# A fused attention and two-layer kernel: three-part storage of the combined weights, a step plan for the output weights and first operands, and the second group's weights fetched first

## The chip, the cores and the metric

One Trainium2 chip, one core. The metric is the device time of one execution in microseconds (us), as the median of several runs. One further execution was taken with the hardware profiler; its rows are the evidence here. Engines: PE is TensorE, ACT is ScalarE, DVE is VectorE, POOL is GpSimd, SP is SyncE, which only issues DMAs here, in the order of the program.

## The reference, cut to what matters

```python
# q, k, v, alpha: (4, 8, 768, 48)
for t in range(S):
    state = alpha[:, :, t, :, None] * state + einsum('bhd,bhe->bhde', k[:, :, t], v[:, :, t])
    y[:, :, t] = einsum('bhd,bhde->bhe', q[:, :, t], state)
x = y.transpose(0, 2, 1, 3).reshape(3072, 384)
h = x @ w_in                                   # w_in (384, 2048)
x = (h * sigmoid(h)) @ w_out                   # w_out (2048, 384)
g = x @ w_gate                                 # w_gate, w_val (384, 1536)
return (g * sigmoid(g) * (x @ w_val)) @ w_out2 # w_out2 (1536, 384)
```

## The kernel before, in words

The 24 chunks of 128 tokens form seven blocks (j = 0 to 6, of 4, 3, 3, 3, 3, 4, 4 chunks). The first layer walks blocks and 16 slices f of w_in and w_out: `g1` makes h of a slice in nine matmuls, `act1` makes silu(h) twice on ACT (`gh`, rounded, and `h`) and DVE forms the remainder `gl`; `g2` multiplies w_out with `gh` (six matmuls) and `gl` (three). PE runs g1 one step ahead of g2: g1(s+1), g2(s), g1(s+2), g2(s+1). A step has two half steps, `slot(s, 0)` before g2 and `slot(s, 1)` after it; hs = 2f + half numbers them in a block. Work for other stages is written into these slots by hand. All engines run their instructions in program order, so an instruction that waits holds up what stands behind it on its engine. Every operand is kept as two float32r parts, high and low; ACT writes a high part, DVE or POOL the low part by subtraction.

The second layer's gate and value products are done as a bilinear scheme: for each of eight groups (NG2 = 8) nine 128x128 weight tiles become 15 combined tiles (5 of part A, 10 of part B), with 15 products per token pair instead of 18. Three pieces of work prepare it, and the change touches all of them.

- **Combined weights** (`combs`, called in each half step of blocks 2 to 5, here a tick; 15 ticks make one group u, k is the tick in it). `load2` brings a raw 64-bit weight unit on SP into one of two raw buffers, `decode2` turns it into float32 on DVE in three instructions (steps 0, 1, 2), `combine` adds tiles on POOL, `high_comb` copies 5 or 10 tiles to a result tile on ACT, `low_comb` makes the remainder on POOL, and `keep_comb` stores the tile to HBM (`comb_d`). All these result tiles of a block share one SBUF buffer, so `high_comb` of one part waits until the store of the part before it has landed. Part A is copied at k = 9 and stored at k = 12; part B is copied at k = 0 of the next group and stored at k = 4.
- **Output weights** (`units_o`, last block, j = 6): 12 units. In one half step DVE decodes a unit, in the next ACT makes the high and POOL the low part; SP stores it in the step after and loads another raw unit behind the store.
- **First operands** (`moving`, last block): 15 operands of 512 tokens for the first token pair from six slices of x: 10 sums (a1 to a10), 15 high copies (h0 to h14) and 15 low parts (l0 to l14). They are taken from the list `MOVING`, two per half step from hs = 5 to 24: sums on POOL, high on ACT, low parts with an odd number on DVE and with an even one on POOL.

`flag` in the last block (hs = 14) sums a range check on PE into PSUM bank 5, DVE copies it to `bad`, and three one-off matmuls (`bits`) then write banks 5, 6 and 7.

The second layer follows an ordered list of events (`GATE`, `VALUE`, due times in the list's own unit). `run(until)` emits the events that are due; near the end of block 6 it is called several times, so that products of group 0 (`p5`, `p0`, `p7` ...; three matmuls each) fall between the last g1 and g2. When block 6 is done, `wstack.close()` frees the first layer's weights, and `fetch(1)`, `fetch(2)`, `fetch(3)` bring the combined weights of groups 1 to 3 into three `ring` buffers that lie in that place. Group 0's were fetched in pieces before (`fetch_first`). The last block's own result goes to HBM (`x1_d`) from `g2` before these fetches are issued.

Of the kernel before, what the change touches and what calls it, by code (L numbers as in the profile page):

```python
# [10 lines left out]
F32 = mybir.dt.float32  # L11
# [9 lines left out]
DM = H * D  # L21
# [247 lines left out]
def fast(ctx, tc, pk, w1, w2, out, bad_i):  # L269
# [464 lines left out]

    def g2(j, f):
# [114 lines left out]
    comb_a, comb_b = {}, {}  # L850

    def high_comb(u, j, keep, n, src):
        t = big((0, 2, 1)[j % 3], f"comb{u}_{n}", F32R)[:, :2 * n * 128]
        t = keep[u] = t.rearrange("p (x i e) -> p x i e", x=2, i=n)
        ACT.activation(out=t[:, 0], in_=src, func=AF.Copy)

    def low_comb(t, src, lo, hi):
        sub(POOL, t[:, 1, lo:hi], src[:, lo:hi], t[:, 0, lo:hi])

    def keep_comb(u, t, lo, hi):  # L860
        SP.dma_start(
            out=comb_d[u, :, 128 * lo:128 * hi], in_=t.bitcast(F32).rearrange("p x i e -> p (x i e)")
        )

    comb_tick = [0]

    def combs(j):

        t, comb_tick[0] = comb_tick[0], comb_tick[0] + 1
        u, k = divmod(t, 15)  # L870
        if t == 0:
            load2(0)
            load2(1)
        if 0 < u <= NG2:
            if k == 0:
                high_comb(u - 1, j, comb_b, 10, fcomb)
            if 1 <= k <= 3:
                low_comb(comb_b[u - 1], fcomb, *((0, 3), (3, 6), (6, 10))[k - 1])
            if k == 4:
                keep_comb(u - 1, comb_b.pop(u - 1), 10, 30)  # L880
        if u >= NG2:
            return
        if k < 9:
            decode2(3 * u + k // 3, k % 3)
# [4 lines left out]
        if k == 9:  # L889
            high_comb(u, j, comb_a, 5, fa[:, :5])  # L890
        for name in {6: ("b1", "b2"), 7: ("b3", "b4"), 8: ("b5",), 9: ("c1", "c2"), 11: ("c3",),
                     12: ("c4", "c5"), 13: ("c6", "c7"), 14: ("c8", "c9")}.get(k, ()):
            combine(name)
        if k == 10:
            low_comb(comb_a[u], fa, 0, 3)
        if k == 11:
            low_comb(comb_a[u], fa, 3, 5)
        if k == 12:
            keep_comb(u, comb_a.pop(u), 0, 10)


    wo_tick, wo_raw, wo_t = [0], [], {}

    def units_o():

        t, wo_tick[0] = wo_tick[0], wo_tick[0] + 1
        f, k = divmod(t, 2)
        key = "2", NW + f
        if t == 0:
            area = big(1, "wo", F32R).rearrange("p (i c) -> p i c", i=4)  # L910
            wo_raw.extend(raw2 + [area[:, i].bitcast(I32) for i in (2, 3)])
            wo_t.update({i: area[:, i] for i in range(2)})
            for i in range(4):
                load_unit(("2", NW + i), w2_src(NW + i), wo_raw[i])
        if k == 0 and 0 < f <= NF2:
            SP.dma_start(out=wo_d[f - 1], in_=wo_t[(f - 1) % 2].bitcast(F32))
            if f + 3 < NF2:
                load_unit(("2", NW + f + 3), w2_src(NW + f + 3), wo_raw[(f + 3) % 4])
        if f >= NF2:
            return  # L920
        if k == 0:
            for i in range(3):
                decode_unit(key, i)
        else:
            to = wo_t[f % 2]
            ACT.activation(out=to[:, :DM], in_=raw_t[key], func=AF.Copy)
            sub(POOL, to[:, DM:], raw_t.pop(key), to[:, :DM])

# [6 lines left out]
    def fetch(n):  # L935
# [4 lines left out]
        if i < NG2:  # L940
            SP.dma_start(out=t.bitcast(F32), in_=comb_d[i])
            a = t[:, :10 * 128].rearrange("p (x i e) -> p x i e", x=2, i=5)
            b = t[:, 10 * 128:].rearrange("p (x i e) -> p x i e", x=2, i=10)
            comb_t[p, i] = lambda x, r: a[:, x, PART_A[r]] if r in PART_A else b[:, x, PART_B[r]]
# [15 lines left out]

    first_comb = {}

    def fetch_first(k):
        src = comb_d[0]
        if k == 0:
            t = first_comb[0] = cw.tile([128, 10, 128], F32R, tag="fcomb", name="first0")
            SP.dma_start(
                out=t.bitcast(F32).rearrange("p i e -> p (i e)"), in_=src[:, :10 * 128]
            )
        elif k == 1:  # L970
            t = first_comb[1] = mp.tile([128, 2, 4, 128], F32R, tag="y3", name="first1", bufs=1)
            for x in range(2):
                lo = (10 + 10 * x) * 128
                SP.dma_start(
                    out=t[:, x].bitcast(F32).rearrange("p i e -> p (i e)"), in_=src[:, lo:lo + 4 * 128]
                )
        else:
            for x in range(2):
                t = first_comb[2 + x] = cw.tile(
                    [128, 6, 128], F32R, tag=f"raw2_{x}", name=f"first{2 + x}"  # L980
                )
                lo = (14 + 10 * x) * 128
                SP.dma_start(
                    out=t.bitcast(F32).rearrange("p i e -> p (i e)"), in_=src[:, lo:lo + 6 * 128]
                )

    def first_view(x, r):
        if r in PART_A:
            return first_comb[0][:, 5 * x + PART_A[r]]
        i = PART_B[r]  # L990
        return first_comb[1][:, x, i] if i < 4 else first_comb[2 + x][:, i - 4]
# [158 lines left out]
    events.sort(key=lambda e: e[0])  # L1150

# [172 lines left out]
    def start_phase2():  # L1324
# [3 lines left out]
        assert comb_tick[0] > 15 * NG2 + 3  # L1328
# [19 lines left out]
    def flag():  # L1348
# [5 lines left out]
        for i in (5, 6, 7):  # L1354
            PE.matmul(
                bank(i, f"bits{i}"), part(unit_t["1", 2 * NF1 - 1], 0), x_t[NB1 - 1][:, 0, 0],
                start=True, stop=True,
            )

    def slot(s, half, first=None):  # L1360
# [24 lines left out]
        if j == NB1 - 1:  # L1385
            units_o()
# [6 lines left out]
            if hs == 26:  # L1393
# [8 lines left out]
    todo = [op for op, _ in MOVING]  # L1402
# [7 lines left out]
    for s, (j, f) in enumerate(steps):  # L1410
# [20 lines left out]
    for n in range(1, 4):  # L1431
        fetch(n)
# [86 lines left out]
```

## Time and profile before

| what | value |
|---|---|
| time before, median of 3 runs | 994.44 us (991.08 to 996.62) |
| the profiled execution, time | 992.06 us |
| its span (first to last instruction) | 990.3 us |
| mean granted TensorE clock | 0.980 |
| busy PE / DVE / ACT / POOL | 930.5 / 623.0 / 449.1 / 319.3 us |

The profiled execution lies 2.4 us below the median of the runs. Times in rows count from the start of the span. PE is busy 94% of the span, so what can be won lies in its idle time and in the stretches in which it ran at a lower clock. A row of idle time names what ended it, which is the last of a chain and not always its cause.

### The profile page before, as it was taken

What the parts mean: (1) busy time and instruction counts of PE and PEld (TensorE: products, weight loads), DVE (VectorE), ACT (ScalarE), POOL (GpSimd) and SP (SyncE); (2) the same over time, 40 slices, a digit from 0 to 9 for tenths busy, and PEclk for the clock granted to TensorE, in tenths of its full rate; (3) what the DMA queues carried; (4) which work ended last, traced back from release to release, by engine and by line L of the source; (5) the groups of instructions that cost most, each with busy time, mean ns of one, the idle gap of its engine ahead of it and who ended that gap; (6) DMA issues with size and microseconds to landing.
All of it is one profiled execution on the core that took longest, in us unless ns stands there. A gap on an engine that the chain in (4) does not pass through costs nothing. (4 is left out here: it accounts for less than half of the span.)

```text
span 990.3 us, 14368 instructions
## 1 busy us (share of the span) xinstructions
PE 930.5 (94%) x5211; PEld 785.2 (79%) x5211; DVE 623.0 (63%) x1075; ACT 449.1 (45%) x1011; POOL 319.3 (32%) x433
## 2 busy tenths in 40 slices
PE   9889999999898999999995969999999999999997
PEld 5667888789897998888884758887888878888786
DVE  8889936556475477466245526687557786476832
ACT  3544435645454455455334324454444453544432
POOL 5344416527576688677315600000000000000000
PEclk9999999999998999999998989999999999999999
DMA  7763202243543454452273254651375632654501
GB/s 242 265 233 95 74 1 99 80 138 105 183 152 120 148 188 162 135 177 81 96 278 131 102 208 190 232 218 45 112 271 204 257 112 80 232 225 165 191 1 67
DMA packets 40558, 150.88 MB, mean 152 GB/s; under 512 B 4128, under 2 KB 7968, under 8 KB 36512
## 3 DMA queue, kind: packets, MB, share of 16 engines
q1 hardware_dynamic: 39856, 149.30, 43.2%
q8 instruction: 43, 0.70, 0.3%
q10 hardware_dynamic: 624, 0.59, 0.2%
q14 instruction: 35, 0.29, 0.1%
HBM read 118.03 MB, written 29.88 MB: 149 GB/s over the span
## 5 line engine op out<-in xcount | busy, mean ns | idle before, releaser
L322 DVE TENSOR_TENSOR gl<-h,gh 128x384 fp32r<-128x384 f32 (+1 forms) x112 | 68.3, 610 | 126.4 <-ACT h L727 125.8
L752 PE MATMUL x<-gh,w 128*128 128x384 f32 (+1 forms) x336 | 124.8, 371 | 9.8 <-ACT gh L726 7.9
L709 PE MATMUL h<-x,w 128*128 128x384 f32 (+1 forms) x336 | 123.9, 369 | 1.8 <-DMA x<-y 1.7
L753 PE MATMUL x<-gh,w 128*128 128x384 f32 (+1 forms) x336 | 123.2, 367 | 0.0
L710 PE MATMUL h<-x,w 128*128 128x384 f32 (+1 forms) x336 | 122.0, 363 | 0.0
L726 ACT ACTIVATE gh<-h 128x384 fp32r<-128x384 f32 (+1 forms) x112 | 59.4, 530 | 92.8 <-PE h L712 92.7
L755 PE MATMUL x<-gl,w 128*128 128x384 f32 (+1 forms) x336 | 85.9, 363 | 4.1 <-DVE gl L322 4.1
L1106 PE MATMUL o<-gh,ring 128*128 128x512 f32 x288 | 88.8, 389 | 0.0
L712 PE MATMUL h<-x,w 128*128 128x384 f32 (+1 forms) x336 | 85.7, 363 | 0.0
L752 PEld LDWEIGHTS x<-gh,w 128*128 128x128 f32 x336 | 64.9, 193 | 20.0 <-ACT gh L726 12.1
L709 PEld LDWEIGHTS h<-x,w 128*128 128x128 f32 x336 | 63.8, 190 | 11.0 <-issue 5.9
L755 PEld LDWEIGHTS x<-gl,w 128*128 128x128 f32 x336 | 61.3, 189 | 13.8 <-DVE gl L322 7.8
L753 PEld LDWEIGHTS x<-gh,w 128*128 128x128 f32 x336 | 64.6, 192 | 5.2
L411 POOL TENSOR_TENSOR kq<-in,r 128x256 f32<-128x256 f32 x47 | 43.8, 932 | 75.5 <-DVE r L400 71.6
L710 PEld LDWEIGHTS h<-x,w 128*128 128x128 f32 x336 | 64.0, 190 | 5.1
L712 PEld LDWEIGHTS h<-x,w 128*128 128x128 f32 x336 | 62.5, 191 | 5.9
L1043 PE MATMUL A<-mov,ring 128*128 128x512 f32 x207 | 59.0, 394 | 8.0 <-DMA ring<-comb_d 8.0
L1106 PEld LDWEIGHTS o<-gh,ring 128*128 128x128 f32 x288 | 54.1, 188 | 11.2
L727 ACT ACTIVATE h<-h 128x384 f32<-128x384 f32 (+1 forms) x112 | 59.5, 532 | 0.0
L1043 PE MATMUL D<-mov,ring 128*128 128x512 f32 x207 | 58.1, 389 | 0.0
L1043 PE MATMUL E<-mov,ring 128*128 128x512 f32 x207 | 58.1, 389 | 0.0
L1106 PE MATMUL o<-gl,ring 128*128 128x512 f32 x144 | 56.3, 391 | 0.8 <-DVE gl L322 0.8
(188 smaller groups left out, 1986.0 us busy)
## 6 DMA issues: line engine op xcount, KB each, us to landing
ring<-comb_d SPq DMA_DIRECT2D x23, 1920.0 KB, 7.6
raw<-in_w_dram SPq DMA_DIRECT2D x58, 384.0 KB, 4.8
in<-in_pk_dram SPq DMA_DIRECT2D x22, 770.5 KB, 4.4
ring<-wo_d SPq DMA_DIRECT2D x6, 1920.0 KB, 7.2
comb_d<-comb SPq DMA_DIRECT2D x8, 1280.0 KB, 6.1
in_v<-in_pk_dram SPq DMA_DIRECT2D x24, 256.0 KB, 3.5
comb_d<-comb SPq DMA_DIRECT2D x8, 640.0 KB, 4.9
x1r<-x_d SPq DMA_DIRECT2D x6, 768.0 KB, 8.8
```

The costliest lines, as they stand in the source:

```text
L322: eng.tensor_tensor(out=lo, in0=src, in1=hi.bitcast(F32), op=ALU.subtract)
L411: KF(d).tensor_tensor(out=kq_t[d][:, 0], in0=in_t[n][1][:, 0, ps_], in1=r_t[d][:, :, 1:], op=ALU.mult)
L709: PE.matmul(acc, part(u, k), xh, start=(k == 0), stop=False)
L710: PE.matmul(acc, part(u, k, 1), xh, start=False, stop=False)
L712: PE.matmul(acc, part(u, k), xl, start=False, stop=(k == len(xk) - 1))
L726: ACT.activation(out=gh, in_=hb, func=AF.Silu)
L727: ACT.activation(out=hb, in_=hb, func=AF.Silu)
L752: PE.matmul(x1_t[j][m], part(u, m), gh, start=(f == 0), stop=False)
L753: PE.matmul(x1_t[j][m], part(u, m, 1), gh, start=False, stop=False)
L755: PE.matmul(x1_t[j][m], part(u, m), gl, start=False, stop=(f == NF1 - 1))
L1043: PE.matmul(acc, s(hs, r), x[:, hx], start=op in new and i == 0, stop=i == 2, skip_group_check=True,)
L1106: PE.matmul(o_t[b][m], part(ring_t[p, f], m, l), x, start=(f == 0 and i == 0), stop=(f == NF2 - 1 and i == 2),)
```

## The change

1. **Combined weights in three parts.** Part B is split in two (7 and 3 tiles). Within a group's row of `comb_d` the three parts lie side by side. In SBUF a block has one area of 24 tiles, which part 0 (10 tiles with its low half) and part 1 (14) fill side by side; part 2 (6 tiles) lies on part 0's place. Part 0 is copied at k = 10 and stored at k = 13; parts 1 and 2 are copied at k = 1 and k = 2 of the next group and stored at k = 4 and k = 5. The decode steps follow a table over k = 0 to 9, loads and combines move by a tick at most. At k = 4 the store now stands ahead of the load on SP; before, the load was issued at k = 3.
2. **Output weights by steps.** One call per step: store of unit f-2, load of unit f+2, high and low part of f-1, decode of f. The first two loads are issued at the end of `combs`.
3. **First operands by steps.** A fixed plan of eight steps (hs = 6 to 20): sums, l14 and l8 on POOL, the other 13 low parts on DVE.
4. `bits` no longer writes bank 5.
5. **Order at the end.** Group 0's events from `p7` on are emitted only after block 6; `fetch(1)` is issued ahead of the last block's store to `x1_d`, which comes next, then `fetch(2)` and `fetch(3)`.

```diff
+    last_x1 = []
+    def keep_x1():
+        out_, in_ = last_x1.pop()
+        SP.dma_start(out=out_, in_=in_)
...
-            SP.dma_start(out=x1_d[:, :, t0:t0 + w], in_=ev[:, :, :w])
+            last_x1.append((x1_d[:, :, t0:t0 + w], ev[:, :, :w]))
+            if j < NB1 - 1:
+                keep_x1()
...
+    CHUNKS = ((0, 0, 5, 0), (10, 0, 7, 10), (24, 7, 10, 0))
+    area_t, keep_t = {}, {}
+    def high_comb(u, j, i):
+        _, lo, hi, at = CHUNKS[i]
+        if j not in area_t:
+            area_t[j] = big((0, 2, 1)[j % 3], f"area{j}", F32R)
+        t = area_t[j][:, 128 * at:128 * (at + 2 * (hi - lo))]
+        t = keep_t[u, i] = t.rearrange("p (x i e) -> p x i e", x=2, i=hi - lo)
+        ACT.activation(out=t[:, 0], in_=(fcomb if i else fa)[:, lo:hi], func=AF.Copy)
...
+    STEPS = {0: (0, 0), 1: (0, 1), 2: (1, 0), 3: (0, 2), 4: (1, 1), 5: (1, 2), 7: (2, 0), 8: (2, 1), 9: (2, 2)}
...
-            if k == 0:
-                high_comb(u - 1, j, comb_b, 10, fcomb)
-            if 1 <= k <= 3:
-                low_comb(comb_b[u - 1], fcomb, *((0, 3), (3, 6), (6, 10))[k - 1])
-            if k == 4:
-                keep_comb(u - 1, comb_b.pop(u - 1), 10, 30)
+            if k in (1, 2):
+                high_comb(u - 1, j, k)
+            if 2 <= k <= 4:
+                low_comb(u - 1, *((1, 0, 3), (1, 3, 7), (2, 7, 10))[k - 2])
+            if k in (4, 5):
+                keep_comb(u - 1, k - 3)
...
-        if k == 3:
+        if k == 4:
             load2(3 * u + 2)
...
-        if k in (9, 12) and u + 1 < NG2:
-            load2(3 * u + 3 + (k == 12))
+        if k in (10, 13):
+            if u + 1 < NG2:
+                load2(3 * u + 3 + (k == 13))
+            else:
+                load_wo(int(k == 13))
...
+    def units_o(f):
+        if f == 0:
+            area = big(1, "wo", F32R).rearrange("p (i c) -> p i c", i=4)
...
+            load_wo(2)
+            load_wo(3)
+        if 2 <= f < NF2 + 2:
+            SP.dma_start(out=wo_d[f - 2], in_=wo_t[f % 2].bitcast(F32))
+            if f + 2 < NF2:
+                load_wo(f + 2)
+        if 1 <= f <= NF2:
+            to, raw = wo_t[(f - 1) % 2], raw_t.pop(("2", NW + f - 1))
+            ACT.activation(out=to[:, :DM], in_=raw, func=AF.Copy)
+            sub(POOL, to[:, DM:], raw, to[:, :DM])
+        if f < NF2:
             for i in range(3):
+                decode_unit(("2", NW + f), i)
...
+    FIRST = (
+        ("h5", "h9", "l5", "l9", "a1", "a2"), ("h7", "h6", "l7", "l6", "a4", "a3"),
+        ("h0", "h14", "l0", "a5", "l14"), ("h12", "h8", "l12", "a6", "l8"),
+        ("h10", "h4", "l4", "a7", "l10"), ("h13", "h2", "l2", "a8", "l13"),
+        ("h3", "l3", "a10", "a9"), ("h11", "h1", "l11", "l1"),
+    )
...
+    early = dict(GATE)["p7"]
...
-        for i in (5, 6, 7):
+        for i in (6, 7):
...
-            if 5 <= hs < 26:
-                for op in todo[2 * hs - 10:2 * hs - 8]:
-                    moving(0, op, None if op[0] == "l" and int(op[1:]) % 2 else POOL)
+            if hs % 2 == 0 and 0 <= hs // 2 - 3 < len(FIRST):
+                for n, op in enumerate(FIRST[hs // 2 - 3]):
+                    moving(0, op, POOL if op[0] == "a" or op in ("l14", "l8") else DVE)
...
-                run(OUTPUT[n] - PAIR)
+                run(min(OUTPUT[n] - PAIR, early))
...
-            run(OUTPUT[min(n + 1, 23)] - PAIR)
+            run(min(OUTPUT[min(n + 1, 23)] - PAIR, early))
...
-    for n in range(1, 4):
-        fetch(n)
+    fetch(1)
+    keep_x1()
+    fetch(2)
+    fetch(3)
```

## Rows read from the trace of the kernel before

**Rows 1.** The waits of PE over the span: total us, times, longest us.
```profile
PE yd L562 <- ACT kt L529: 4.7, 1, 4.7
```
**Rows 2.** Busy us by stretch: PE, PEld, DVE, ACT, POOL; granted clock, DMA share, GB/s.
```profile
525.00:550.00 25.00, 13.78 (x48) 11.00 (x48) 8.87 (x13) 9.44 (x18) 15.65 (x13) 0.80 0.44 147
...
575.00:600.00 25.00, 16.97 (x67) 13.58 (x66) 5.47 (x8) 6.03 (x11) 0.00 (x0) 0.80 0.64 257
```
**Rows 3.** PE by time, layers' seam: start us, us, operation, count, [idle us before, releaser].
```profile
582.23 0.84 PE L1043 MATMUL B<-mov,first 128*128 128x512 f32 x3
582.91 0.84 PE L1043 MATMUL D<-mov,first 128*128 128x512 f32 x3
...
592.47 1.62 PE L1043 MATMUL A<-mov,ring 128*128 128x512 f32 x3 [8.03 <-DMA ring<-comb_d]
...
596.44 0.97 PE L1043 MATMUL A<-mov,ring 128*128 128x512 f32 x3
```
**Rows 4.** SP's DMA issues in order of time there, and landing of the ring's fetches.
```profile
583.09 0.58 SPq L764 DMA_DIRECT2D x_d<-x1e  x1
583.77 2.13 SPq L941 DMA_DIRECT2D ring<-comb_d  x3
...
DMA to landing us min/median/max: 6.9/7.6/17.3
```
**Rows 5.** PE in order of time in the last block: its two long waits and their restart.
```profile
528.46 0.80 PE L752 MATMUL x<-gh,w 128*128 128x512 f32 x1 [3.30 <-ACT gh L726]
...
531.19 1.15 PE L755 MATMUL x<-gl,w 128*128 128x512 f32 x3
...
542.44 1.65 PE L1355 MATMUL bits<-x,w 128*128 128x512 f32 x3 [7.92 <-DVE bad L1352]
...
545.55 0.40 PE L752 MATMUL x<-gh,w 128*128 128x512 f32 x1
```
**Rows 6.** ACT in order of time ahead of these waits.
```profile
527.29 0.63 ACT L799 ACTIVATE mov<-x1r 128x512 fp32r<-128x512 f32 x1 [2.40 <-POOL x1r L794]
...
537.51 0.54 ACT L926 ACTIVATE wo<-wo 128x384 fp32r<-128x384 f32 x1 [2.71 <-DVE wo L103]
```
**Rows 7.** DVE in order of time: decode alone and beside POOL, low parts.
```profile
529.54 0.35 DVE L93 TENSOR_SCALAR dec<-raw 128x384 int32<-128x384 int32 x1
529.92 0.56 DVE L98 SCALAR_TENSOR_TENSOR raw<-raw,dec 128x384 int32<-128x384 int32 x1
...
532.72 0.69 DVE L322 TENSOR_TENSOR gl<-h,gh 128x512 fp32r<-128x512 f32 x1 [1.64 <-ACT h L727]
...
534.39 1.51 DVE L98 SCALAR_TENSOR_TENSOR wo<-wo,dec 128x384 int32<-128x384 int32 x1
```
**Rows 8.** POOL in order of time there.
```profile
531.84 1.04 POOL L322 TENSOR_TENSOR wo<-raw,wo 128x384 fp32r<-128x384 f32 x1 [4.58 <-issue]
532.84 1.30 POOL L794 TENSOR_TENSOR x1r<-x1r 128x512 f32<-128x512 f32 x1
534.09 1.39 POOL L322 TENSOR_TENSOR mov<-x1r,mov 128x512 fp32r<-128x512 f32 x1
```
**Rows 9.** Combined weights: ACT's waits from 225 to 500 us, and its copies of part B.
```profile
ACT comb L855 <- DMA comb_d<-comb: 17.4, 4, 8.2
...
L855 ACT ACTIVATE comb<-fcomb x8: 1261/1272/1278, 240.7 to 485.0; 128x1280 fp32r<-128x1280 f32 x8
```
**Rows 10.** Around the longest: ACT, and the granted clock in ten microseconds.
```profile
308.12 1.27 ACT L855 ACTIVATE comb<-fcomb 128x1280 fp32r<-128x1280 f32 x1 [8.25 <-DMA comb_d<-comb]
...
310.00:320.00 10.00, 9.63 (x55) 9.18 (x56) 6.69 (x15) 4.45 (x16) 7.36 (x8) 0.66 0.21 67
```
**Rows 11.** A raw weight that came late: DVE, then PE, then PE's clock.
```profile
256.85 0.36 DVE L93 TENSOR_SCALAR dec<-raw 128x384 int32<-128x384 int32 x1 [3.17 <-DMA raw<-in_w_dram]
...
257.60 0.44 PE L550 MATMUL yd<-pt,in_v 128*64 128x128 f32 x4 [2.52 <-DVE pt L520]
...
259.00:260.00 1.00, 1.00 (x10) 0.82 (x4) 0.06 (x1) 1.00 (x4) 1.00 (x3) 0.50 0.52 100
```

More of the change, by code (lines that the diff above doesn't have):

```diff
@@ L848, in combine, with low_comb, keep_comb @@
         )
[L850 to L860, printed above, removed]
+    CHUNKS = ((0, 0, 5, 0), (10, 0, 7, 10), (24, 7, 10, 0))
[7 more added lines that the diff above has]
+        ACT.activation(out=t[:, 0], in_=(fcomb if i else fa)[:, lo:hi], func=AF.Copy)
+    def low_comb(u, i, lo, hi):
+        t, first = keep_t[u, i], CHUNKS[i][1]
+        sub(POOL, t[:, 1, lo - first:hi - first], (fcomb if i else fa)[:, lo:hi], t[:, 0, lo - first:hi - first])
+    def keep_comb(u, i):
+        to, lo, hi, _ = CHUNKS[i]
         SP.dma_start(
-            out=comb_d[u, :, 128 * lo:128 * hi], in_=t.bitcast(F32).rearrange("p x i e -> p (x i e)")
+            out=comb_d[u, :, 128 * to:128 * (to + 2 * (hi - lo))],
+            in_=keep_t.pop((u, i)).bitcast(F32).rearrange("p x i e -> p (x i e)"),
         )
     comb_tick = [0]
+    STEPS = {0: (0, 0), 1: (0, 1), 2: (1, 0), 3: (0, 2), 4: (1, 1), 5: (1, 2), 7: (2, 0), 8: (2, 1), 9: (2, 2)}
+    TERMS = {6: ("b1", "b2"), 7: ("b3", "b4"), 8: ("b5",), 10: ("c1", "c2"), 11: ("c3", "c4"),
+             12: ("c5",), 13: ("c6", "c7"), 14: ("c8", "c9")}
     def combs(j):
@@ L881, in combs @@
         if u >= NG2:
             return
-        if k < 9:
-            decode2(3 * u + k // 3, k % 3)
-        if k == 3:
+        if k in STEPS:
+            i, step = STEPS[k]
+            decode2(3 * u + i, step)
+        if k == 4:
             load2(3 * u + 2)
-        if k in (9, 12) and u + 1 < NG2:
-            load2(3 * u + 3 + (k == 12))
[L889 to L892, printed above, removed]
-            combine(name)
@@ L894, in combs @@
[L894 to L909, printed above, removed]
+        if k in (10, 13):
[3 more added lines that the diff above has]
+                load_wo(int(k == 13))
@@ L910, in units_o, with load_wo @@
+        if k == 10:
+            high_comb(u, j, 0)
+        if k in (11, 12):
+            low_comb(u, 0, *((0, 3), (3, 5))[k - 11])
+        for name in TERMS.get(k, ()):
+            combine(name)
+        if k == 13:
+            keep_comb(u, 0)
+    wo_raw, wo_t = list(raw2), {}
+    def load_wo(f):
+        load_unit(("2", NW + f), w2_src(NW + f), wo_raw[f % 4])
+    def units_o(f):
+        if f == 0:
             area = big(1, "wo", F32R).rearrange("p (i c) -> p i c", i=4)
-            wo_raw.extend(raw2 + [area[:, i].bitcast(I32) for i in (2, 3)])
+            wo_raw.extend(area[:, i].bitcast(I32) for i in (2, 3))
@@ L912, in units_o @@
             wo_t.update({i: area[:, i] for i in range(2)})
[L913 to L921, printed above, removed]
-            for i in range(3):
[L923 to L927, printed above, removed]
+            load_wo(2)
@@ L931, in fast, with tile_at @@
+    FIRST = (
[4 rows of a table added]
+    )
+    def tile_at(x, r):
+        if r in PART_A:
+            return 5 * x + PART_A[r]
+        i = PART_B[r]
+        return 10 + 7 * x + i if i < 7 else 24 + 3 * x + i - 7
     items = [(p, i) for p in range(NPAIR) for i in range(NG2 + 3)]
@@ L941, in fetch @@
             SP.dma_start(out=t.bitcast(F32), in_=comb_d[i])
-            a = t[:, :10 * 128].rearrange("p (x i e) -> p x i e", x=2, i=5)
-            b = t[:, 10 * 128:].rearrange("p (x i e) -> p x i e", x=2, i=10)
-            comb_t[p, i] = lambda x, r: a[:, x, PART_A[r]] if r in PART_A else b[:, x, PART_B[r]]
+            v = t.rearrange("p (n e) -> p n e", e=128)
+            comb_t[p, i] = lambda x, r: v[:, tile_at(x, r)]
         else:
@@ L963, in fetch_first @@
     def fetch_first(k):
-        src = comb_d[0]
         if k == 0:
-            t = first_comb[0] = cw.tile([128, 10, 128], F32R, tag="fcomb", name="first0")
+            parts = [(cw.tile([128, 10, 128], F32R, tag="fcomb", name="first0"), 0)]
+        elif k == 1:
+            parts = [(mp.tile([128, 8, 128], F32R, tag="y3", name="first1", bufs=1), 10)]
+        else:
+            parts = [
+                (cw.tile([128, 6, 128], F32R, tag=f"raw2_{x}", name=f"first{2 + x}"), 18 + 6 * x)
+                for x in range(2)
+            ]
+        for t, lo in parts:
+            n = t.shape[1]
             SP.dma_start(
-                out=t.bitcast(F32).rearrange("p i e -> p (i e)"), in_=src[:, :10 * 128]
+                out=t.bitcast(F32).rearrange("p i e -> p (i e)"), in_=comb_d[0, :, 128 * lo:128 * (lo + n)]
             )
[L970 to L985, printed above, removed]
+            for i in range(n):
+                first_comb[lo + i] = t[:, i]
     def first_view(x, r):
[L988 to L991, printed above, removed]
+        return first_comb[tile_at(x, r)]
     comb_t[0, 0] = first_view
@@ L1326, in start_phase2 @@
         pools2["s"] = ctx.enter_context(tc.tile_pool(name="sp2", bufs=2))
-        assert comb_tick[0] > 15 * NG2 + 3
         small = mp.tile([128, 2 * 512], F32, tag="y3", name="small", bufs=1)
@@ L1385, in slot @@
         if j == NB1 - 1:
-            units_o()
+            if hs % 2 == 0:
+                units_o(hs // 2)
             if hs == 1:
@@ L1392, in slot @@
                 fetch_first(1)
-            if hs == 26:
+            if hs == 24:
                 fetch_first(2)
```

1 line of the change is left out of this document (removed).

## The prediction, made before the change was run

> **What bounds the kernel now.** I read the waits of PE first. The two longest of the run, 8.03 and 7.92 us, stand in the stretch that the change rewrites [rows 3, 5]; the next, 4.7 us for ACT's `kt`, belongs to the combined weights [rows 1]. The stretches then show the size: of the 50 us in 525 to 550 and 575 to 600 PE is busy for 30.75 us, and its granted clock averages 0.80 in both, against 0.980 over the run [rows 2]. PE by time gives each wait and its restart.
>
> The seam of the layers: the last products of group 0 that are in line end at 584.4 us, and the next product needs the ring of group 1, which comes 8.03 us later; the first nine matmuls then take 3.97 us (592.47 to 596.44) where three take 0.68 us at the full clock, so 1.9 us more go to the lower clock (1.2 instead of 2.4 GHz) [rows 3]. SP shows why the ring is late: its fetch is issued at 583.77, behind the store of the last block's result at 583.09, which itself had to wait for that result to be copied [rows 4].
>
> In the last block PE waits 3.30 us for `gh` and 7.92 us for `bad`. Six matmuls after the first take 2.73 us instead of 1.36, seven after the second 3.11 instead of 1.59: 2.9 us more at the lower clock [rows 5]. Neither wait is PE's or the flag's own doing: ACT reached silu late because a high copy ahead of it waited 2.40 us for a sum on POOL, and because a high part of the output weights waited 2.71 us for DVE's decode [rows 6]. DVE was late because its decode ran beside POOL [rows 7, 8].
>
> In blocks 2 to 5, ACT waits 17.4 us, four times, for a store of combined weights [rows 9]. After the longest, 8.25 us, `kt` is late, PE loses 4.7 us [rows 1, 10], and the clock averages 0.66 over the ten microseconds that follow, 3.4 us more [rows 10].
>
> **The change part by part.** The sum is made against the profiled execution's 992.06 us.
>
> *The seam.* Moving p7, p14, p12 and p2 behind block 6 takes four products, 4 x 0.68 = 2.72 us [rows 3], out of block 6, which then ends at 582.2 - 2.7 = 579.5 on the old axis. PE now has seven products of group 0 after it, 4.8 us, to 584.3. The fetch no longer waits for the copy and the store; at the latest it goes out when block 6's last weights are used, about 579.6, and lands 6.9 us later (the least of 23 fetches [rows 4]; this one has the engines to itself), at 586.5. Group 1 would begin 592.5 - 586.5 = 6.0 us earlier, with a wait of 2.2 us left. If the buffer lies under weights that were used earlier, there is no wait: 592.5 - 584.3 = 8.2 us. The 1.9 us of lower clock go wholly or not at all, since an idle time of 2.52 us was enough for it elsewhere [rows 11]. So 6.0 to 10.1 us; I take the middle, 8. The store now stands ahead of the second ring. Before, the rings of groups 2 and 3 landed at most 583.8 + 2.1 + 17.3 - 592.5 = 10.7 us after the first [rows 3, 4], 5.4 us each; the store has two fifths of a ring's bytes, 2.1 us. So the second ring lands some 7.5 us after the first, and group 2 wants it eleven products, 7.5 us, after. I cost that at nothing; should the cover fall short it is a wait of 1 or 2 us.
>
> *The last block.* Taken away are 3.3 + 7.9 us of waiting and 2.9 us of lower clock, 14.1 us, if ACT and DVE keep up. Dropping bank 5 from `bits` alone would not do it, since silu was held by ACT as well. What speaks for the step plan: each high part follows a decode of the step before, and each high copy a sum of the step before, so ACT need not stand. What speaks against it is DVE. A step of PE is 18 matmuls, 4.08 us at 0.227. In eight steps (32.6 us) DVE has per step a `gl` (0.69) and a decode (0.35 + 0.56 + 0.56 alone), and 13 low parts in all, costed like `gl`, which has their shape [rows 7]: 8 x 2.16 + 9.0 = 26 us. POOL has 8 low parts of weights (1.04), 10 sums (1.30) and 2 low parts (1.39): 24 us [rows 8]. Beside POOL, DVE's decode took 1.51 instead of 0.56 us [rows 7, 8]. If the two never overlapped except in `gl` (which reads PSUM and took 0.69 beside POOL too [rows 7, 8]), 20.8 + 24 = 44.8 us would be wanted in 32.6: 12 us too much, of which the distance from `gl` to its use (nine matmuls of g2, nine of g1 and six of the next g2, 5.4 us, less some 1.2 for ACT and 0.7 for itself: 3.5 us) covers a part, so about 8 us would come back as waits. If they overlapped freely nothing would. POOL often stands waiting for DVE's low parts, so I take 4, and 0.5 for the clock: a gain of 9.6, between 6 and 14. That DVE's fixed decode is in order ahead of `gl` is what makes it late, and the last third of g2 is what would wait.
>
> The Trainium skill ("SBUF — State Buffer", section "Who interferes with whom") says that a DVE instruction with two SBUF inputs or in a two-port mode and a GpSimd instruction that reads SBUF shut each other out for the whole instruction. The rows of DVE beside POOL agree in kind (1.51 for 0.56 us); by that rule the case of no overlap holds, and this term would be 6 instead of 9.6.
>
> *Combined weights.* Seven groups take 485.0 - 240.7 = 244 us, one 35, a tick 2.3 us [rows 9]. Part 1, seven of the ten tiles of part B, no longer waits for the store of part 0. Part 2 does, one tick later in distance (k = 13 to 17 instead of 12 to 15), so the 8.25 us become at most 6, and silu and `kt` get past ahead of it. What can be saved is 4.7 + 3.4 us there, and of the other waits' 17.4 - 8.25 = 9.2 us at the same ratio (4.7 of 8.25) at most 5.2: 13.3 in all. Since the cause stays for part 2, I take 6. Against it: the raw weight of k = 4 stands behind a store of 14 tiles (14/30 of a ring, 2.5 us) that waits for POOL in its turn. One raw weight was late already: DVE stood 3.17 us, PE 2.52 us, and the clock fell to half [rows 11]; with a restart like those of the last block (1.5 us [rows 5]) that is 4 us for one. If two of the other groups come half as late, 3 to 4 us are lost. Net 3, from -6 (nothing saved, one and a half late weights) to +13. ACT pays one more instruction in eight groups, hidden in its idle time (it is busy for 449 of 990 us).
>
> The two early loads of output weights and the table of layouts move no work that PE waits for; I cost them at nothing.
>
> Sum: 8 + 9.6 + 3 = 20.6 us, 992.1 to 971.5. The median of the runs was 2.4 us above the profiled execution, so 974.
>
> **The rivals.**
> First, DVE becomes the bound of the last block: the full 8 us and a clock fall of 2 us come back. Its decode of 1.51 us beside POOL speaks for it, POOL's own waits against. The last block gains 4, the sum 15: 979. The rule of the Trainium skill ("SBUF — State Buffer", "Who interferes with whom") is this case.
>
> Second, the combined weights gain all they can and DVE keeps up: 8 + 14 + 13 = 35 us: 959. For it: the four waits have one cause. Against it: part 2 keeps that cause.
>
> Third, on the other side: the raw weights behind the store. Each group whose raw weight comes as late as in [rows 11] costs 4 us. The gains of the seam and the last block are 17.6 us, so from the fifth group on the kernel is slower, and all seven give 28 - 17.6 = 10 us more than before: 1,005. Against it: the load could never leave before the decode that frees its buffer, which moved by a tick as well, so only the store's 2.5 us come in between.
>
> Fourth, the change does not do what it says: the fetch is still held to about 584 by something at the seam, and another wait on ACT takes the place of the one for `bad`. The combined weights' 3 us are then all: 991.
>
> **How the numbers follow.** Forecast 0.62; DVE as bound 0.17; all gained 0.09; nothing moved 0.07; raw weights late 0.05. The predicted time is the forecast's, 974. For the range I take the second rival's end, less one microsecond, as the low bound, 958, and at the high end the least of the bounds, 6.0 + 6 - 6 = 6 us of gain, 988: this leaves out the last two cases and little else. About 0.5%, 5 us, is what a measurement of this kernel can tell from no change: faster 0.88, same 0.07, slower 0.05.
>
> **What the profile of the changed kernel would show.** Seam: the first ring's fetch ahead of the store, issued within half a microsecond of the end of block 6 or before, and PE's wait for it 0 to 2.5 us. Last block: no wait for `bad`; waits for `gl` in its place, together under 5 us, if DVE is late; clock near 1.00 in that stretch. Combined weights: ACT's wait for their store under half of 17.4 us; DVE's wait for a raw weight tells what it cost. The prediction is wrong if waits for `gl` or `gh` of 8 us and more stand in the last block, if the ring still comes 6 us late, or if DVE stands for raw weights in four groups and more.

## The result, and the profile after

The changed kernel takes 965.91 us (median of 4 runs, 965.36 to 967.4) where the kernel before took 995.5 beside it (4 runs, 991.08 to 996.62): a ratio of 0.9713, 95% interval 0.968 to 0.9746, some 28 us less. The sign was forecast, and the time lies inside the range, but the forecast of 974.0 us was 8 us too high. The profiled execution took 967.4 us, with a span of 965.5 and a mean granted clock of 0.985.

The waits of PE over the whole span of the changed kernel (total us, times, longest), which answer to [rows 1]:
```profile
PE x L761 <- DVE gl L322: 6.1, 12, 1.5
PE yd L550 <- DVE pt L520: 6.1, 3, 4.0
PE A L1066 <- DMA ring<-comb_d: 5.1, 2, 4.9
```
The wait for `bad` [rows 5] and the 4.7 us for `kt` at `yd` [rows 1] are gone. The ring is still waited for, and a wait of 4.0 us for `pt` is new.

Where the 24.8 us of span came from is read off one instruction that marks the end of each block, SP's store of the block's result. It stands at 206.27, 274.89, 346.63, 421.47, 499.35 and 583.09 us before, and after the change at:
```profile
206.03 0.57 SPq L739 DMA_DIRECT2D x_d<-x1e  x1
268.25 0.58 SPq L739 DMA_DIRECT2D x_d<-x1e  x1
338.16 0.58 SPq L739 DMA_DIRECT2D x_d<-x1e  x1
411.39 0.58 SPq L739 DMA_DIRECT2D x_d<-x1e  x1
489.84 0.58 SPq L739 DMA_DIRECT2D x_d<-x1e  x1
...
558.02 0.58 SPq L739 DMA_DIRECT2D x_d<-x1e  x1
```
The reader subtracts neighbours. Blocks 2 to 5, in which the combined weights are made, gained 6.4, 1.8 and 1.6 us and lost 0.6: 9.3 in all. The last block went from 83.74 to 68.18; 2.72 of that are the four products moved out of it, so 12.8 were won. From the store to the first product with a ring it is 592.47 - 583.09 = 9.38 us before and 566.96 - 558.02 = 8.94 after; with the 2.72 moved into this stretch the seam gained 3.2. The second layer behind it took 0.7 more, and the stretch up to 206 us 0.2 less.

The seam after the change, PE in order of time (start us, us, operation, [idle before, releaser]), against [rows 3]:
```profile
557.16 0.84 PE L1066 MATMUL A<-mov,first 128*128 128x512 f32 x3
...
561.25 0.84 PE L1066 MATMUL F<-mov,first 128*128 128x512 f32 x3
566.96 1.62 PE L1066 MATMUL A<-mov,ring 128*128 128x512 f32 x3 [4.88 <-DMA ring<-comb_d]
...
572.17 0.86 PE L1066 MATMUL E<-mov,first 128*128 128x512 f32 x3
```
and SP's issues in order of time, against [rows 4]:
```profile
557.36 0.32 SPq L973 DMA_DIRECT2D ring<-comb_d  x1
558.02 0.58 SPq L739 DMA_DIRECT2D x_d<-x1e  x1
558.65 1.62 SPq L973 DMA_DIRECT2D ring<-comb_d  x2
```
The first fetch does leave at the end of block 6, ahead of the store, as forecast. But PE gets the ring 566.96 - 557.36 = 9.6 us after the issue (its landing is at 9.5), not 6.9, still stands 4.88 us, and restarts at 1.62 us for three matmuls where 0.84 is usual: the lower clock was not escaped. Before, with the store issued 0.68 us ahead of it, the fetch was used 592.47 - 583.77 = 8.7 us after its issue [rows 3, 4]: the place ahead of the store won an earlier issue, and part of that went into a longer transfer.

The last block by stretch (busy us of PE, PEld, DVE, ACT, POOL; clock, DMA share, GB/s), against the first row of [rows 2], and its only two waits of PE, against [rows 5]:
```profile
500.00:525.00 25.00, 25.00 (x113) 20.69 (x112) 23.40 (x28) 12.76 (x25) 15.32 (x12) 1.00 0.59 210
525.00:550.00 25.00, 22.53 (x97) 17.68 (x96) 21.39 (x29) 13.53 (x25) 15.30 (x12) 1.00 0.55 195
```
```profile
530.32 0.96 PE L761 MATMUL x<-gl,w 128*128 128x512 f32 x3 [0.85 <-DVE gl L322]
540.71 0.97 PE L761 MATMUL x<-gl,w 128*128 128x512 f32 x3 [1.54 <-DVE gl L322]
```
DVE is busy for 44.8 of 50 us, and 2.4 us of `gl` waits take the place of 11.2 us of idle time and a restart at 1.2 GHz; the clock stays at its full 2.4 GHz.

In the blocks before, ACT's waits for the stores of combined weights fall from 17.4 us [rows 9] to 5.0 (3.4 for its own stores, 1.6 for the block's). What replaces them is seen on DVE, PE, SP and the clock, against [rows 10, 11]:
```profile
ACT area L868 <- DMA comb_d<-area: 3.4, 2, 2.6
...
ACT area L868 <- DMA x_d<-x1e: 1.6, 1, 1.6
```
```profile
285.67 0.36 DVE L93 TENSOR_SCALAR dec<-raw 128x384 int32<-128x384 int32 x1 [5.50 <-DMA raw<-in_w_dram]
285.94 0.42 DVE L520 TENSOR_TENSOR pt<-s,mask 128x256 f32<-128x256 f32 x1
```
```profile
286.42 0.69 PE L550 MATMUL yd<-pt,in_v 128*64 128x128 f32 x4 [4.02 <-DVE pt L520]
```
```profile
277.58 0.38 SPq L876 DMA_DIRECT2D comb_d<-area  x1
278.06 0.38 SPq L677 DMA_DIRECT2D raw<-in_w_dram  x1
```
```profile
280.00:290.00 10.00, 5.98 (x60) 5.04 (x60) 2.72 (x8) 3.11 (x10) 5.38 (x10) 0.77 0.65 233
290.00:300.00 10.00, 10.00 (x54) 10.00 (x54) 5.02 (x13) 5.47 (x16) 6.25 (x11) 0.89 0.20 54
```
The raw weights leave behind the 14-tile store and are used 7.6 us after their issue (285.67 - 278.06), where the page of the profile gives 4.9 us from issue to landing as the median of 58 such loads. DVE stands 5.50 us, `pt` is queued right behind, PE stands 4.02 us for it, and the clock drops. At 255 us DVE waits too (2.36 us), and PE does not: that is taken up below.

### The profile page after: what moved, and what is told of

Same layout as the page of the kernel before. It is cut to its first block, busy times and chain, and to the rows that moved or that the text cites. A ratio compares the mean times of both kernels' runs of the same rounds, so it can differ in the third digit from the quotient of the medians.

```text
span 965.5 us, 14386 instructions
## 1 busy us (share of the span) xinstructions
PE 926.9 (96%) x5210; PEld 784.1 (81%) x5210; DVE 630.7 (65%) x1081; ACT 451.6 (47%) x1019; POOL 315.2 (33%) x427
## 3 DMA queue, kind: packets, MB, share of 16 engines
q1 hardware_dynamic: 40864, 149.30, 44.8%
## 4 chain that ended last, share of the span: by engine, by line
PE 74%; DVE 10%; issue 5%; DMA 4%; ACT 3%; POOL 2%; SPq 1%; POOLq 0%; DVEq 0%; ACTq 0%
PE o L1129 15%; PE h L709 5%; PE A L1066 5%; PE h L712 5%; PE h L710 5%; PE x L761 5%; PE D L1066 5%; PE x L759 5%; PE x L758 5%; PE E L1066 5%; DMA ring<-comb_d 2%; PE yd L550 2%; PE G L1066 2%; POOL w L322 2%; PE K L1066 2%
## 5 line engine op out<-in xcount | busy, mean ns | idle before, releaser
L758 PE MATMUL x<-gh,w 128*128 128x384 f32 (+1 forms) x336 | 122.4, 364 | 1.4 <-ACT gh L726 1.3
L759 PE MATMUL x<-gh,w 128*128 128x384 f32 (+1 forms) x336 | 121.8, 362 | 0.0
L761 PEld LDWEIGHTS x<-gl,w 128*128 128x128 f32 x336 | 60.9, 189 | 16.8 <-DVE gl L322 11.2
L758 PEld LDWEIGHTS x<-gh,w 128*128 128x128 f32 x336 | 63.5, 189 | 8.9 <-ACT gh L726 3.5
L759 PEld LDWEIGHTS x<-gh,w 128*128 128x128 f32 x336 | 63.6, 189 | 5.2
L1129 PEld LDWEIGHTS o<-gh,ring 128*128 128x128 f32 x288 | 54.1, 188 | 11.2
L322 DVE TENSOR_TENSOR gl<-a,gh 128x512 fp32r<-128x512 f32 x48 | 32.8, 691 | 37.3 <-ACT gh L1118 36.2
```

What stands on the lines that cost most here:

```text
L322: eng.tensor_tensor(out=lo, in0=src, in1=hi.bitcast(F32), op=ALU.subtract)
L758: PE.matmul(x1_t[j][m], part(u, m), gh, start=(f == 0), stop=False)
L759: PE.matmul(x1_t[j][m], part(u, m, 1), gh, start=False, stop=False)
L761: PE.matmul(x1_t[j][m], part(u, m), gl, start=False, stop=(f == NF1 - 1))
L1129: PE.matmul(o_t[b][m], part(ring_t[p, f], m, l), x, start=(f == 0 and i == 0), stop=(f == NF2 - 1 and i == 2),)
```

## The experiments

Ratios are to the kernel before, which ran on the same chip beside each (median 994.2, 994.1 and 993.9 us in the three sets), with 95% intervals. The changed kernel's 0.9713 is 965.7 us on that scale.

**One part at a time, in the kernel before.** The first has only the fifth item of the change:
```diff
+    fetch(1)
+    keep_x1()
+    fetch(2)
+    fetch(3)
```
(with `min(..., early)` in `run`, and `keep_x1`).

> The kernel before with the seam alone changed: group 0's events from p7 on after block 6, the first ring's fetch ahead of the last block's store. Theory (the store and the next two rings, issued right behind it, share the DMA engines with the first ring): the ring lands 9 to 10 us after its issue, PE waits 4 to 5.5 us for it instead of 8.0, and the gain is 2.5 to 5 us. Rival (the prediction's term: a ring at the head of the queue has the engines to itself): it lands after 6.9 us, PE waits at most 2.5 us, and the gain is 6 to 10 us.

Measured: 991.45 us, 0.9973 (0.9958 to 0.9987). SP issues the fetch at 580.39 and PE starts on it 9.6 us later:
```profile
589.99 1.62 PE L1051 MATMUL A<-mov,ring 128*128 128x512 f32 x3 [4.87 <-DMA ring<-comb_d]
```
The seam by itself is worth 2.7 us, not 8, and the late landing is not a side effect of the other parts.

The second has the output weights and first operands by steps, and `bits` without bank 5:
```diff
+            if hs % 2 == 0:
+                units_o(hs // 2)
...
+            if hs % 2 == 0 and 0 <= hs // 2 - 3 < len(FIRST):
...
-        for i in (5, 6, 7):
+        for i in (6, 7):
```

> The kernel before with the last block alone changed: output weights and first operands by the fixed plan of steps, bits on banks 6 and 7 only, all four first loads of output weights in the last block. Theory (the waits came from ACT and DVE standing in turn; DVE beside POOL gives back 2 to 3 us): gain 10 to 14 us, PE waits for gl of 1 to 4 us, none over 3 us. Rival (DVE shut out by POOL becomes the bound): waits for gl of about 8 us, gain 4 to 7 us.

Measured: 980.5 us, 0.9863 (0.9841 to 0.9885): 13.6 us. Its PE waits for `gl` total 5.8 us over the whole run, as in the full change, with none above 1.5.

The third has the combined weights in three parts alone:
```diff
+    CHUNKS = ((0, 0, 5, 0), (10, 0, 7, 10), (24, 7, 10, 0))
...
-        if k == 3:
+        if k == 4:
             load2(3 * u + 2)
```

> The kernel before with the combined weights alone changed: three parts, new ticks, the load behind the store at k = 4. Theory (what is taken from ACT's wait for the store is worth more than the late raw weights cost): ACT waits under 6 us for stores instead of 17.4, gain 5 to 11 us. Rival (the prediction's term): gain 3 us, since raw weights behind the store take half of it back; DVE stands for raw weights in three groups or more.

Measured: 985.31 us, 0.9899 (0.9876 to 0.9922): 10.0 us. ACT waits 3.6 us for its stores instead of 17.4, and DVE's late raw weights come with the part:
```profile
286.43 0.36 DVE L93 TENSOR_SCALAR dec<-raw 128x384 int32<-128x384 int32 x1 [5.53 <-DMA raw<-in_w_dram]
```
The three parts together give 2.7 + 13.6 + 10.0 = 26.3 us, the whole 28.5: within the intervals they add.

The fourth drops only bank 5 from `bits`:
```diff
-        for i in (5, 6, 7):
+        for i in (6, 7):
```

> The kernel before, bits no longer writes bank 5. Theory (silu was held by ACT as well): PE waits some 5 us for gh in the place of 7.9 for bad, gain 2 to 4 us. Rival (the flag is the whole cause): the wait is gone, gain 8 to 10 us.

Measured: 989.91 us, 0.9963 (0.9947 to 0.9979). PE in order of time:
```profile
529.84 0.79 PE L752 MATMUL x<-gh,w 128*128 128x512 f32 x1 [3.25 <-ACT gh L726]
541.09 0.50 PE L752 MATMUL x<-gh,w 128*128 128x512 f32 x1 [0.59 <-ACT gh L726]
551.27 0.50 PE L752 MATMUL x<-gh,w 128*128 128x512 f32 x1 [1.73 <-ACT gh L726]
557.97 0.50 PE L752 MATMUL x<-gh,w 128*128 128x512 f32 x1 [2.32 <-ACT gh L726]
```
The 7.92 us for `bad` [rows 5] come back in part as waits for silu (`gh`): over the run these total 12.9 us, where it was 7.9 before. Removing the wait without the step plan gives 3.7 us; the plan gives the other ten of the second experiment.

**What makes the raw weights late.** In the changed kernel, the load is put ahead of the store in the fourth and fifth tick of a group. (The expectations call the block from 268 to 338 us the second block, and a tick a matmul group.)
```diff
-            if k in (4, 5):
+            if u == NG2 and k in (4, 5):
                 keep_comb(u - 1, k - 3)
...
         if k == 4:
             load2(3 * u + 2)
+        if u and k in (4, 5):
+            keep_comb(u - 1, k - 3)
```

> The changed kernel, with one order turned round: at the fourth and fifth matmul group of each block the load of the next raw weights is issued ahead of the store of the combined weights instead of behind it. Theory (the raw weights come late because their load stands behind a store of 14 tiles on one queue): VectorE's waits for the raw weights, 9.2 us in the changed kernel with 5.5 in the second block, fall under 3 us, TensorE's wait of 4.02 us for the decoded weights at 286 us is gone with the lower clock behind it, and the kernel takes 961 us (959 to 963) where the changed kernel takes 965.7. Rival (the transfers share the same engines, so that the order at the queue does not matter): VectorE still waits 7 us or more and the time stays within 2 us of 965.7.

Measured: 962.93 us, 0.9684 (0.9668 to 0.9699). DVE's waits for raw weights from 225 to 500 us fall from 9.2 us to 4.9:
```profile
283.82 0.36 DVE L93 TENSOR_SCALAR dec<-raw 128x384 int32<-128x384 int32 x1 [3.79 <-DMA raw<-in_w_dram]
```
```profile
284.57 0.69 PE L550 MATMUL yd<-pt,in_v 128*64 128x128 f32 x4 [2.31 <-DVE pt L520]
```
```profile
277.44 0.39 SPq L677 DMA_DIRECT2D raw<-in_w_dram  x1
```
The interval overlaps the changed kernel's, so the trace has to decide. Both theories were half right: the use comes 1.85 us earlier, 0.6 of it because the load leaves earlier, but it still takes 6.4 us. The 14-tile store behind it cannot be the whole reason. Later in the same run a raw load has a store of the same size 0.43 us behind it and lands 3.9 us after its issue. Two things differ: the load of the next inputs (770 KB) left 0.42 us ahead here and 2.92 us ahead there, and the store of part 2 left 0.7 us behind the first store here and 4.7 us behind it there:
```profile
277.02 0.33 SPq L365 DMA_DIRECT2D in<-in_pk_dram  x1
277.92 1.04 SPq L876 DMA_DIRECT2D comb_d<-area  x2
...
370.40 0.33 SPq L365 DMA_DIRECT2D in<-in_pk_dram  x1
373.32 0.33 SPq L677 DMA_DIRECT2D raw<-in_w_dram  x1
373.75 5.09 SPq L876 DMA_DIRECT2D comb_d<-area  x2
```
With nothing issued close by, such a load lands after 2.9 to 3.1 us. With an input load 0.44 us ahead and no store near (at 397.67 in the kernel before) it takes 4.7; with a 14-tile store 0.43 us ahead and no input load close (at 375.67 and 449.11 in the changed kernel) 4.8 and 4.9; the one at 278.06, with both ahead and part 2's store behind, 7.6. So the store is a part of what makes this load late, and the input load another. That is a comparison of loads within runs; no experiment moved the input load.

**Whether DVE and POOL shut each other out in the last block.** The ten sums go from POOL to DVE:
```diff
-  moving(0, op, POOL if op[0] == "a" or op in ("l14", "l8") else DVE)
+  moving(0, op, POOL if op in ("l14", "l8") else DVE)
```

> The changed kernel, with the ten sums of first operands in the last block moved from POOL to VectorE. Theory (each of the two engines stretches the other's work while both run, which made the decode 1.5 us in place of 0.56): the decodes shrink, TensorE's waits for the output weights in the last block, 2.4 us, vanish, and the time is 963 to 965 us. Rival (VectorE just has too much work in this stretch, and ten more sums make it later): the waits for the output weights grow to 5 us or more and the time is 968 to 972 us.

Measured: 966.63 us, 0.9723 (0.9707 to 0.9739), not to be told from the changed kernel. The decode of the output weights from 507 to 546 us, by groups, in the changed kernel:
```profile
L98 DVE SCALAR_TENSOR_TENSOR raw<-raw,dec 128x384 int32<-128x384 int32 x4 | 5.5, 1386 | 0.2
...
L93 DVE TENSOR_SCALAR dec<-raw 128x384 int32<-128x384 int32 x4 | 3.6, 908 | 0.0
```
and with the sums on DVE:
```profile
L98 DVE SCALAR_TENSOR_TENSOR raw<-raw,dec 128x384 int32<-128x384 int32 x4 | 3.2, 789 | 0.4
...
L93 DVE TENSOR_SCALAR dec<-raw 128x384 int32<-128x384 int32 x4 | 1.4, 345 | 0.0
```
POOL does stretch DVE's decode (908 against 345 ns, 1386 against 789). But PE's waits for `gl` between 500 and 550 us only go from 2.4 to 1.7 us, and the block from 68.18 to 67.84 (489.72 to 557.56). The stretching is shown. It cannot cost the kernel much, since PE waits only 2.4 us for `gl` in this block. How much of these is due to it the run does not tell: DVE took over 9.1 us of sums, and its busy time in the block went only from 51.5 to 50.4 us. The rival that ten more instructions make DVE late is refuted.

**What makes the first ring late.** In one kernel the ring goes out alone and everything else 5 us later on ACT's queue; in the other the three rings go out together and only the store is late.
The ring alone:
```diff
     fetch(1)
+    run(dict(GATE)["u0"] + 0.01)
+    later.append(ACT)
     fetch(2)
+    keep_x1()
     fetch(3)
```

> The changed kernel, with the first ring of combined weights issued alone at the end of the last block; the block's store and the other two rings are issued about 5 us later, by ScalarE's queue. Theory (the first ring lands 9.5 us after its issue, not 6.9, because the store and the two rings share its engines): it lands 6.9 to 7.5 us after its issue, TensorE's wait of 4.88 us for it falls to 2 to 2.8, and the time is 961 to 964 us. Rival (the ring needs 9.5 us by itself, as a transfer of this form): TensorE still waits 4.5 us or more, and the time is 965.7 us or more, since the later rings come later too.

Only the store late:
```diff
     fetch(1)
     fetch(2)
     fetch(3)
+    run(dict(GATE)["u0"] + 0.01)
+    keep_x1(ACT)
```

> The changed kernel, with the three rings issued one behind the other at the end of the last block as before, and only the block's store moved behind them, about 5 us later. If the store is what delays the first ring: it lands 7 to 7.5 us after its issue, TensorE waits 2 to 3 us, and the time is 962 to 964 us. If it is the second and third ring: it lands 9 us or more after its issue, the wait stays above 4.3 us, and the time stays within 1.5 us of 965.7.

Measured: 963.93 us, 0.9696 (0.9678 to 0.9715), and 964.39 us, 0.9706 (0.9681 to 0.973). The intervals overlap with the changed kernel's, so the times alone decide little; the traces do. The ring alone, issued at 556.82:
```profile
564.47 1.50 PE L1066 MATMUL A<-mov,ring 128*128 128x512 f32 x3 [2.93 <-DMA ring<-comb_d]
```
Only the store late, issued at 556.34:
```profile
564.35 1.62 PE L1066 MATMUL A<-mov,ring 128*128 128x512 f32 x3 [3.29 <-DMA ring<-comb_d]
```
From issue to use it is 7.65 us alone (nothing else is issued for 4.8 us behind it), 8.0 beside the other rings, and 9.6 with the store in between: of the 1.95 us lost to company the store takes 1.6. The other 0.35 are hardly more than what the fetch alone varies by: it takes 7.75 and 7.89 us in the two kernels below. Even alone, the ring needs more than the 6.9 us forecast (it lands after 7.5), PE stands some 3 us, and the lower clock stays.

**Together, and the load a tick earlier.** First both orders turned (the fifth and the seventh experiment in one kernel), then, in that kernel, also
```diff
-        if k == 4:
+        if k == 3:
             load2(3 * u + 2)
```

> Both turned orders together in the changed kernel: the raw weights' load ahead of the combined weights' store, and the first ring alone, with the last block's store and the other rings 5 us later. If the two gains stand in different stretches and add (3.0 and 2.0 us by their own runs): 960.9 us (959.5 to 962.3). If what is won in the blocks is only waited out at the seam, or the other way round: 962.5 us or more.

> As the kernel with both orders turned, and the third raw load of each block issued at the third matmul group instead of the fourth, as soon as its buffer is free, so that it has a whole group's time ahead of the store. Theory (what is left of VectorE's waits, 3.79 us in the second block, is the load sharing the engines with the 14-tile store behind it): that wait falls under 1.5 us, TensorE's 2.31 us for the decoded weights go, and the time is 957.5 to 959.5 us. Rival (the load is slow because of the other loads of the block, whatever stands behind it): the wait stays above 3 us less the earlier issue's 4 us, TensorE's wait is filled by another of the second block, and the time stays at 960 to 962 us.

Measured: 961.87 us, 0.9663 (0.9644 to 0.9683): the two gains add, as far as the interval can tell. And 956.87 us, 0.9623 (0.9606 to 0.964): 4 us more by the ratios and 5 by the medians, a little beyond the expected 957.5 to 959.5, and faster than both kernels. Its trace, by SP and by stretch:
```profile
274.83 0.33 SPq L677 DMA_DIRECT2D raw<-in_w_dram  x1
...
277.65 1.50 SPq L876 DMA_DIRECT2D comb_d<-area  x2
```
```profile
280.00:290.00 10.00, 10.00 (x95) 9.51 (x94) 6.61 (x17) 6.00 (x18) 7.87 (x12) 1.00 0.70 230
290.00:300.00 10.00, 10.00 (x93) 9.70 (x95) 6.66 (x13) 5.99 (x18) 9.69 (x16) 1.00 0.50 156
```
The load leaves 2.8 us ahead of the store, as soon as the decode that frees its buffer has ended (273.18 + 1.63 = 274.81), lands 3.1 us after its issue, and is used at 280.17 without a wait. It now also leaves 2.4 us ahead of the input load (277.23), so this run shows that a head start takes the wait away, and not that the store alone had caused it, as the theory says. DVE's waits for raw weights from 225 to 500 us are 0.7 us now, and PE is busy throughout, at the full clock. The block from 268.33 to 331.39 takes 63.06 us instead of 69.91.

## Why the prediction was right in sign and 8 us too high

Of the 8 us, the terms account for 4.1: the sum gave 971.5 for a profiled execution, which then took 967.4. The other 3.9 are scatter between the profiled executions and the medians (2.4 us below the median before, 1.5 above it after). Within the sum, errors of opposite sign met: the seam was put 4.8 us too high, the last block 3.2 and the combined weights 6.3 too low. That the sum came so near is in part luck.

**The seam: 8 forecast, 3.2 in the trace, 2.7 alone.** The order and the moment of issue came out as written. The step that failed is the landing: "lands 6.9 us later (... this one has the engines to itself)". It did not have them: the store and two rings were issued within 2.9 us behind it. The 6.9 was the least of 23 fetches, and the fetch alone took 7.65. The cost of the store was looked for at the second ring; it fell on the first, which had been issued ahead of it. The Trainium skill ("DMA: Bandwidth & Descriptors", section "Queues, rings and completion order") says that an engine consumes a ring's descriptors in order, while a later transfer may finish writing before an earlier one. Here the store landed behind the fetch (10.8 us after its own issue, against 9.5), so no run shows the second half. The 9.6, 8.0 and 7.65 us show that being first in the queue does not protect a fetch from the store behind it. With it fell the bound: 6.0 us were called the least, and the 2.7 us of later landing are what is missing from them. The 8 itself was the middle between 6.0 and the 10.1 of an earlier issue; the fetch left 0.2 us after the last matmuls of block 6 (557.36, 557.16), so that the lower case held. The 1.9 us of lower clock, which were to go "wholly or not at all", did not go: the fifth product starts 572.17 - 566.96 = 5.21 us after the restart, where the full clock would give 4 x 0.68 = 2.72 and the kernel before took 4.78. The 0.4 us between the two need not come from the change: in the second, third and fourth experiment, which left the seam as it was, the same stretch took 4.73, 5.25 and 4.61 us.

**The last block: 9.6 forecast, 12.8 in the trace, 13.6 alone** (interval 11.4 to 15.8). The mechanism was right in each part: no wait for `bad`, waits for `gl` in its place, clock 1.00. Only sizes were off: 4.5 us of giving-back were charged, and 2.5 came; and 14.1 us were taken away, where it was 15.3. The block by itself, before and after, gives the account (from store to store; busy PE first, then the other engines and the clock):
```profile
499.35:583.09 83.74, 71.82 (x301) 58.22 (x300) 42.33 (x62) 32.81 (x63) 35.69 (x30) 0.94 0.47 165
...
489.84:558.02 68.18, 65.71 (x288) 53.47 (x287) 51.52 (x66) 32.75 (x61) 31.64 (x24) 1.00 0.55 191
```
Idle time fell from 11.92 to 2.47 us, 9.45; PE's busy time fell by 6.11, of which 2.72 are the moved products and 3.39 the lower clock. Two shorter waits for `gh` (0.7 us together) and 0.5 us of lower clock had been left out of the 14.1. "Neither wait is PE's or the flag's own doing" was too strong: 3.7 of the 13.6 us come from the bank alone, as the fourth experiment shows. The first rival (DVE becomes the bound; 979 us) had the mechanism, not the consequence: DVE is stretched by POOL, as the sixth experiment shows, but PE waits only 2.4 us for `gl`. Taking 14.6 us of sums from POOL, at the price of 9.1 us on DVE, moved the block by 0.3 us. The rule of the Trainium skill ("SBUF — State Buffer", section "Who interferes with whom") agrees in kind with the decode's 908 and 345 ns; the time that was worked out from it did not come.

**The combined weights: 3 forecast, 9.3 in the trace, 10.0 alone.** This is the term that was off most, and in both its halves. Where it has 6 saved and 3 lost, some 16 were saved and 7 lost. The kernel with the earlier load gives the yardstick: its four blocks take 62.22, 63.06, 70.93 and 78.43 us; the changed kernel's 62.22, 69.91, 73.23 and 78.45; those before 68.62, 71.74, 74.84 and 77.88. So the late raw weights cost the change 6.85 us in one block, where one wait of DVE stands for 4.02 us of PE, and the other 2.8 go with the lower clock behind it. The 2.3 us of the next block (73.23 and 70.93) are not theirs: DVE waits there 0.49 us for a raw weight in the changed kernel and 0.53 in the faster one; PE's wait for `kt` is 0.8 us shorter and the clock 1.00 instead of 0.98, and with the same order of load and store that block took 71.24 us in the fifth experiment and 73.66 in the ninth. What sets it stays open. The third rival had the place, and the store as a part of the mechanism; the price was higher (4 us for one had been charged), but it fell due in one block, where the input load stood close ahead too, and not in all groups, so that it could not turn the sign. Its counter-argument, "the load could never leave before the decode that frees its buffer", named the right limit; the load stood 3 us behind that limit, and moving it up to it took the cost away.

The saved half failed at two steps. One is "Since the cause stays for part 2, I take 6": ACT's waits for its own stores went from 17.4 to 3.4 us, and in the kernel with the earlier load the block of the longest one takes 8.7 us less (71.74 to 63.06), the 4.7 and 3.4 us of the prediction and a little more. The other is a wait that the prediction had read [rows 11] and used only as a price. In block 2 the change gained 6.4 us, although DVE's wait for a raw weight is still there (2.36 us at 255.34; 3.17 before). Before, `pt` was queued behind the waiting decode (257.13, 0.42 us), and PE waited for `pt`. In the new table of steps `pt` has run already, at 251.10, and what stands behind the decode is this:
```profile
255.34 0.42 DVE L93 TENSOR_SCALAR dec<-raw 128x384 int32<-128x384 int32 x1 [2.36 <-DMA raw<-in_w_dram]
255.68 0.55 DVE L322 TENSOR_TENSOR x<-yd,x 128x384 fp32r<-128x384 f32 x1
```
In the kernel with the early load that same `x` starts at 255.30 and waits for ACT, with no late weight ahead of it. So the wait costs nothing there, while before it cost PE 2.52 us and a restart at the lower clock [rows 11], which shows as 2.6 us more of busy time in that block (64.81 and 62.22): 5.1 of the 6.4 us. The other 1.3 are a wait of PE for `kt` at 248.39 that is gone. This is read from the two traces; no experiment moved that instruction alone. The prediction's list of signs had "DVE stands for raw weights in four groups and more" as a sign against the forecast: DVE does stand five times from 225 to 500 us, for 9.2 us, and most of the cost hangs on one of them. How often it stands was the wrong thing to count.

**The rivals.** All gained (959): the last block kept up and the blocks came near it, the seam did not. Nothing moved (991): refuted.

## What to carry to other kernels

A transfer's price is its landing in the company in which it will run: take the landing of one that had the same traffic issued around it, and give a load that is waited for a head start over the large transfers around it (here a store and a 770 KB load), not only the place ahead of them. For a wait on an in-order engine, read which instruction is queued behind it and who waits for that: with `pt` ahead of the late decode its wait cost PE nothing, where it had cost some 5 us, and its load one tick earlier was worth 4 to 5 us. An engine that is stretched by another costs only what its consumer then waits.

## What the runs showed that was not expected

While the store at the seam is served, the transfers together move much less. All transfers of the four microseconds around PE's wait, in the changed kernel (562 to 566 us) and, in the second fence, with only the store moved away (560 to 564 us):
```profile
DMA packets 219, 1.04 MB, mean 259 GB/s; under 512 B 15, under 2 KB 15, under 8 KB 172
```
```profile
DMA packets 128, 1.72 MB, mean 430 GB/s; under 512 B 16, under 2 KB 16, under 8 KB 16
```
With the store there, 172 of 219 packets are under 8 KB, and the rate is 259 GB/s instead of 430, though the engines' busy share, by single microseconds, is 0.73 to 1.11 there and 0.93 to 1.08 without the store. The small packets themselves are not what is slow: from 562 to 564 us the rate is 215 GB/s with none of them, and from 566 to 567 us, when 192 of 197 packets are small, it is 458. What makes the rate low before they come was not tried. Open as well: what shortens the block after the late weight by 2.3 us in some of the kernels, and how long the lower clock lasts at the seam (4.25 to 5.26 us to the fifth product over all twelve kernels, in no order of the wait before it: 5.26 after 3.16 us, 4.61 after 8.13).
